# Decoding the second network's weights one unit at a time over the experts, its last matrix inside the second network, and the experts' token transposes in two PSUM buffers

## The chip, the cores and the metric

One NeuronCore of one Trainium2 chip runs the whole program. The metric is the device time of one execution in microseconds (us). The engines are PE (TensorE, matrix products), DVE (VectorE), ACT (ScalarE), POOL (GpSimd) and SP, which here only issues DMAs. SBUF is the on-chip memory, PSUM the memory that PE writes, in banks of 512 floats per partition.

## The reference, cut to what matters

```python
for t in range(S):                                     # gated linear attention, 4 x 8 heads, 768 tokens
    state = alpha[:, :, t, :, None] * state + outer(k[:, :, t], v[:, :, t])
    y[:, :, t] = q[:, :, t] @ state
x = y as 3072 rows of 384
chosen = x @ w_skip > 0                                # only these rows go to an expert
e_idx = argmax(x @ w_gate); gate_w = its softmax       # one of 8 experts
x[chosen] += gate_w * (relu(x @ w1[e]) @ w2[e])        # 384 -> 1024 -> 384
h = maximum(maximum(x @ w1, x @ w2), x @ w3)           # second network, 384 -> 768
return h @ w_out                                       # 768 -> 384
```

All of it is in float32. A product is made of three matmuls, with each operand split into a high and a low part.

## The kernel before

**Three stages.** The first stage (0 to 147.55 us) computes the attention and the routing and scatters the chosen tokens into slots of their experts. The experts' stage (147.55 to 317.14 us) takes 8 experts with 256 slots each. The second network (317.14 us to the end) takes all 3072 tokens in 6 groups of 512.

**The experts' loop** runs over s = 0 to 65. The expert is e = s // 8 and the step in it f = s % 8, called "step 0" to "step 7" here. A step does, in this order in every engine's queue: one generator step of the weight decoding (`mdecs`), the split of the expert weights for the step three ahead (`wsplit`: ACT writes wh, L99; then DVE or POOL writes wl, L100; POOL at steps 1, 3 and 6, DVE at the others), the first product (`gemm1`: 9 matmuls, L618 to L620, into PSUM tile ph; ACT writes hh, L623; DVE writes hl, L624) and the second product of two steps earlier (`gemm2`: 6 matmuls, L636 to L638). At step 1 the `gemm2` of the expert before ends: DVE writes o twice (L645) and POOL scatters it by two indirect DMAs (L646). At steps 4, 5 and 6 `xprep` transposes a third of the next expert's tokens on PE (k = 0, 1, 2; L606, two matmuls), then ACT writes xh (L99) and DVE xl (L100).

**PSUM in this stage**: `ps_t` has one buffer, for the transposes (pt); `ps_h` has three, which ph takes in turn; `ps_o` has two. A new tile waits until the readers of the tile that had its buffer are done. For ph and pt the last reader is the DVE operation that writes hl or xl.

**The decoding.** The four matrices of the second network come as 64-bit integers' words in 8 loads (`mload`, tile rm). Each load holds two units of 128 x 576, so a matrix has four units and there are 16. A unit takes `decode_abs` on ACT (L80), `decode_exp` on DVE (L84, L85), `decode_bits` on DVE (L90, L91), a copy to the high part mh on ACT (L580 or L586) and the low part ml on POOL (L583 or L588). With each expert from 3 on, the two units of one load are decoded over steps 0 to 6, interleaved: exp of the first unit at step 1, its bits at step 2, exp of the second at step 3, its bits at step 4, the copies at 3 and 5, the low parts at 4 and 6.

**The end of the experts.** `select` and `merge` add expert 7's output to the first token group, with three one-hot tiles kept in the rm buffers.

**The second network** does for each group g and slice f (6 of them) `gemm1`: 27 matmuls (L772 to L774) into three ph tiles; ACT copies the first (L787), DVE takes the maximum with the other two (L789), ACT writes hh and DVE hl. Its `gemm2` (12 matmuls, L804 to L806, with the last matrix mh[3], ml[3]) follows one slice later. At slices 2 to 4 `gtr` transposes the next group.

**Routing of the last tokens.** Generators `rA` (4 chunks) and `rB` (2 chunks) are advanced by `stage`. Their last part sums the softmax on DVE (L394 to L396) and scatters by indirect DMA on POOL (L399).

Of the kernel before, what the change touches and what calls it, by code (L numbers as in the profile page):

```python
# [44 lines left out]
DEC = 3  # L45
LEAD = 3
WS = 5
HALF = 1
XL = 6
XP = 4  # L50
IX = 6
MF = True
ML = 2
FIRST = (0, 6, 2)
KEEP = (0, 6)
GT = 512
# [7 lines left out]
def tile_gla_moe_moe2(ctx, tc, akq, vp, rp, wgt, cst, io, ew, md, out):  # L64
# [14 lines left out]
    def decode_abs(t, raw):  # L79
        A.activation(t, words(raw)[1], AF.Abs)  # L80
# [21 lines left out]
    with tc.manual_schedule():  # L102
# [427 lines left out]
               ps_s.tile([128, NP, C], F32, name="ps0").rearrange("p a b -> p (a b)")[:, 0:CAP]]  # L530
        gather(0, 3)
        stage(rB)
        gather(3, 4)
        for k in range(k3):
            for m in range(2):
# [1 line left out]
                         start=False, stop=False)  # L537
        stage(rB)
        gather(4, NC)
        stage(rA)  # L540
        stage(rB)
        xs_, xh_, xl_, ix_ = {}, {}, {}, {}
        xh_[0] = xhp.tile([128, k3, CAP], F32R, name="xh")
# [7 lines left out]
        mh = [m2p.tile([128, 2304], F32R, name=f"mh{i}") for i in range(4)]  # L551
        ml = [m2p.tile([128, 2304], F32R, name=f"ml{i}") for i in range(4)]

        ls = ExitStack()
        xp = pool("xp", 2, reuse_waits="tile")
        hq = pool("hq", LAG + 2, reuse_waits="tile")
# [4 lines left out]
        rm = {}  # L561

        def mload(e):
            rm[e] = xp.tile([128, 4 * UN], F32, name="rm")
            SY.dma_start(out=rm[e].bitcast(I32), in_=md[e].bitcast(I32))

        def mdecs(e):
            ts = [xp.tile([128, UN], F32, name="dt") for u in range(2)]
            raw = [rm[e][:, 2 * UN * u:2 * UN * (u + 1)] for u in range(2)]
            zs = [slice((2 * (e % 2) + u) * UN, (2 * (e % 2) + u + 1) * UN) for u in range(2)]  # L570
            h = [mh[e // 2][:, z] for z in zs]
            l = [ml[e // 2][:, z] for z in zs]
            decode_abs(ts[0], raw[0])
            yield
            decode_exp(ts[0])
            decode_abs(ts[1], raw[1])
            yield
            decode_bits(ts[0], raw[0])
            yield
            A.copy(h[0], ts[0])  # L580
            decode_exp(ts[1])
            yield
            G.tensor_tensor(l[0], ts[0], h[0].bitcast(F32), ALU.subtract)  # L583
            decode_bits(ts[1], raw[1])
            yield
            A.copy(h[1], ts[1])  # L586
            yield
            G.tensor_tensor(l[1], ts[1], h[1].bitcast(F32), ALU.subtract)  # L588
            yield

        def xload(e):
            xs_[e] = xp.tile([128, 2, XW], F32, name="xs", bufs=3)
# [2 lines left out]
        def xprep(e, k):  # L595
            xs = xs_[e]
            if k < 0:
                ix_[e] = xp.tile([128, 2, 1], I32, name="ix", bufs=4)
                V.tensor_copy(ix_[e], xs[:, :, DM + 1:DM + 2])
                return  # L600
            if k == 0:
                xh_[e] = xhp.tile([128, k3, CAP], F32R, name="xh")
                xl_[e] = xhp.tile([128, k3, CAP], F32R, name="xl")
            pt = bank(ps_t, "pt")[:, 0:CAP]
            for m in range(2):
                T.transpose(pt[:, m * 128:(m + 1) * 128], xs[:, m, k * 128:(k + 1) * 128], ident)  # L606
            split(xh_[e][:, k, :], xl_[e][:, k, :], pt)
# [65 lines left out]
                         start=(c == 0), stop=False)  # L673

        def select():
            rm_ = [xp.tile([128, 4 * UN], F32, name="rm") for i in range(2)]
            pair = lambda i, a, w: rm_[i][:, a:a + 2 * w].rearrange("p (m d) -> p m d", m=2).bitcast(F32R)
            p7, yh, yl = pair(0, 0, GT), pair(0, 2 * GT, DM), pair(1, 0, DM)
            for m in range(2):
                V.tensor_scalar(p7[:, m, :], iota, xs_[NE - 1][:, m, DM + 1:DM + 2], None, ALU.is_equal)  # L680
            t = rawp.tile([128, 8 * DM], F32, name="raw").bitcast(F32R)
            xh_[0], xl_[0] = (t[:, i * 4 * DM:(i + 1) * 4 * DM].rearrange("p (k t) -> p k t", k=k3) for i in range(2))
            return p7, yh, yl

        def merge():
            e = NE - 1
            p7, yh, yl = sel
            for m in range(2):
                A.activation(yh[:, m], po_[e][m], AF.Copy, scale=xs_[e][:, m, DM:DM + 1])
                V.scalar_tensor_tensor(yl[:, m], po_[e][m], xs_[e][:, m, DM:DM + 1], yh[:, m].bitcast(F32),  # L690
                                       ALU.mult, ALU.subtract)
            for k in range(k3):
                z = slice(k * 128, (k + 1) * 128)
                for i in range(4):
                    T.matmul(pm[k], (yh, yl)[i // 2][:, i % 2, z], p7[:, i % 2, :], start=False, stop=(i == 3))
                split(xh_[0][:, k, :], xl_[0][:, k, :], pm[k])

        xg_ = {}
# [11 lines left out]
            V.tensor_tensor(chk[:, 7:8], chk[:, 5:6], chk[:, 6:7], ALU.mult)  # L710
            V.tensor_copy(okb, chk[:, 7:8])

        if MF:
            mload(0)
        ns = NE * nf1
        dg = [mdecs(e) for e in range(NE)]
        for s in range(ns + LAG):
            e, f = divmod(s, nf1)
            for d in range(NE):
                if s >= d * nf1 + max(DEC - d, 0):  # L720
                    next(dg[d], None)
            if s < ns:
                if 4 <= s + AHEAD < ns:
                    wsplit(s + AHEAD, V if f in (0, 2, 4, 5, 7) or s < 2 else G)
                if s and (s + AHEAD) % 4 == 3 and (s + AHEAD) // 4 + 2 < 2 * NE:
                    wload((s + AHEAD) // 4 + 2)
                if f == XL and e + 2 < NE:
                    xload(e + 2)
                if s == 0:
                    xload(1)  # L730
                    xload(0)
                    if not MF:
                        mload(0)
                if f == ML and e + 1 < NE:
                    mload(e + 1)
                gemm1(s)
            if s in (ns - 1, ns):
                gstart(s - ns + 1)
            if s == ns + 1:
                gstart(2)  # L740
            if s >= LAG:
                gemm2(s - LAG)
            x0 = XP if e else 5
            if e + 1 < NE and x0 <= f < x0 + k3:
                xprep(e + 1, f - x0)
            if f == IX and e < NE:
                xprep(e, -1)
# [48 lines left out]
        def gemm2(g, f):  # L796
# [4 lines left out]
            for c in range(4):  # L801
# [5 lines left out]
                if f == nf2 - 1:  # L807
                    o = xp.tile([128, DM], F32, name="o2", bufs=4)
                    A.copy(o, po)
                    SY.dma_start(out=out[g * GT + c * 128:g * GT + (c + 1) * 128, :], in_=o)  # L810

        pend = None
        for g in range(ng):
            for f in range(nf2):
                gemm1(g, f)
                if f == 0 and g + 1 < ng:
                    gload(g + 1)
                if pend is not None:
                    gemm2(*pend)
                pend = (g, f)  # L820
                if g + 1 < ng and 2 <= f < 2 + k3:
                    gtr(g + 1, f - 2)
# [204 lines left out]
```

## Time and profile before

| what | value |
|---|---|
| median of 3 runs | 637.07 us (636.66 to 638.45) |
| the profiled execution | 631.28 us |
| its span, first to last instruction | 629.5 us |
| PE busy, weight load busy | 591.3 us (94%), 528.4 us (84%) |
| DVE busy | 357.9 us (57%) |
| ACT busy, POOL busy | 242.2 us (38%), 174.8 us (28%) |
| mean granted TensorE clock | 0.987 of full speed |

The profiled execution lies 5.8 us below the median of the runs. Busy shares are means over three stages of different nature, so the rows below are taken by stage, by expert and by step. Times in the rows count from the start of the span. The clock column (PEclk) gives the granted share of 2.4 GHz, so 0.50 is the lower level, 1.2 GHz.

### The profile page before, as it was taken

What the parts mean: (1) busy time and instruction counts of PE and PEld (TensorE: products, weight loads), DVE (VectorE), ACT (ScalarE), POOL (GpSimd) and SP (SyncE); (2) the same over time, 40 slices, a digit from 0 to 9 for tenths busy, and PEclk for the clock granted to TensorE, in tenths of its full rate; (3) what the DMA queues carried; (4) which work ended last, traced back from release to release, by engine and by line L of the source; (5) the groups of instructions that cost most, each with busy time, mean ns of one, the idle gap of its engine ahead of it and who ended that gap; (6) DMA issues with size and microseconds to landing.
All of it is one profiled execution on the core that took longest, in us unless ns stands there. A gap on an engine that the chain in (4) does not pass through costs nothing.

```text
span 629.5 us, 10447 instructions
## 1 busy us (share of the span) xinstructions
PE 591.3 (94%) x4103; PEld 528.4 (84%) x4103; DVE 357.9 (57%) x637; ACT 242.2 (38%) x503; POOL 174.8 (28%) x151
## 2 busy tenths in 40 slices
PE   5999898889798988898999999999999999999995
PEld 3898888789798988898888888888888888888884
DVE  6899999877899888988642323322322332232221
ACT  2556566555455766667221221112212212122111
POOL 5544678735455645664310000000000000000000
PEclk8899999999899999999999999999999999999999
DMA  8689796924875756673130011002003001001001
GB/s 331 241 232 344 265 337 253 367 92 173 290 281 210 282 211 254 221 301 113 56 120 1 1 44 57 1 2 100 1 1 100 1 0 51 1 0 51 1 2 55
DMA packets 28667, 85.67 MB, mean 136 GB/s; under 512 B 3234, under 2 KB 20624, under 8 KB 25664
## 3 DMA queue, kind: packets, MB, share of 16 engines
q1 hardware_dynamic: 26048, 80.08, 36.3%
q0 software_dynamic: 2560, 4.83, 2.0%
q8 instruction: 34, 0.56, 0.4%
q14 instruction: 25, 0.20, 0.1%
HBM read 67.47 MB, written 20.49 MB: 140 GB/s over the span
## 4 chain that ended last, share of the span: by engine, by line
PE 68%; DVE 17%; issue 4%; DMA 4%; POOL 3%; ACT 1%; DVEq 0%; POOLq 0%; ACTq 0%; SPq 0%
PE ph L774 12%; PE ph L773 12%; PE ph L772 12%; PE po L806 4%; PE po L804 4%; PE po L805 4%; DVE dt L85 3%; DVE wl L100 3%; PE ph L619 2%; PE ph L620 2%; PE ph L618 2%; DMA akq<-in_akq_dram 2%; DVE sf L203 2%; PE po L638 2%; PE ps L246 2%
## 5 line engine op out<-in xcount | busy, mean ns | idle before, releaser
L789 DVE TENSOR_TENSOR h<-ph,h 128x512 f32<-128x512 f32 x72 | 49.8, 692 | 173.0 <-PE ph L774 172.9
L772 PE MATMUL ph<-xh,mh 128*128 128x512 f32 x270 | 106.3, 394 | 0.0
L774 PE MATMUL ph<-xh,ml 128*128 128x512 f32 x270 | 105.6, 391 | 0.0
L773 PE MATMUL ph<-xl,mh 128*128 128x512 f32 x270 | 105.4, 390 | 0.0
L99 ACT CAST hh<-h 128x512 fp32r<-128x512 f32 x36 | 22.3, 621 | 150.3 <-DVE h L789 150.3
L100 POOL TENSOR_TENSOR wl<-raw,wh 128x768 fp32r<-128x768 f32 x26 | 48.7, 1872 | 43.7 <-ACT wh L99 41.6
L774 PEld LDWEIGHTS ph<-xh,ml 128*128 128x128 f32 x270 | 50.7, 188 | 10.9
L773 PEld LDWEIGHTS ph<-xl,mh 128*128 128x128 f32 x270 | 50.7, 188 | 9.9
L772 PEld LDWEIGHTS ph<-xh,mh 128*128 128x128 f32 x270 | 50.7, 188 | 9.7
L619 PE MATMUL ph<-xl,wh 128*128 128x256 f32 x192 | 55.2, 288 | 2.4 <-DVE xl L100 2.3
L618 PE MATMUL ph<-xh,wh 128*128 128x256 f32 x192 | 57.2, 298 | 0.0
L99 ACT CAST wh<-raw 128x768 fp32r<-128x768 f32 x64 | 53.4, 834 | 8.4 <-PE po L638 7.8
L620 PE MATMUL ph<-xh,wl 128*128 128x256 f32 x192 | 55.1, 287 | 0.0
L787 ACT COPY h<-ph 128x512 f32<-128x512 f32 x36 | 21.1, 587 | 74.3 <-PE ph L774 74.3
L806 PE MATMUL po<-mh,hl 128*128 128x384 f32 x144 | 48.6, 338 | 0.0
L804 PE MATMUL po<-mh,hh 128*128 128x384 f32 x144 | 48.4, 336 | 0.0
L805 PE MATMUL po<-ml,hh 128*128 128x384 f32 x144 | 48.4, 336 | 0.0
L638 PE MATMUL po<-wh,hl 128*128 128x384 f32 x128 | 44.2, 345 | 0.5 <-DVE hl L624 0.5
L636 PE MATMUL po<-wh,hh 128*128 128x384 f32 x128 | 43.9, 343 | 0.0
L637 PE MATMUL po<-wl,hh 128*128 128x384 f32 x128 | 43.7, 341 | 0.0
L246 PE MATMUL ps<-q,k 64*128 64x128 f32 x384 | 31.7, 292 | 12.5 <-POOL q L221 9.8
L100 DVE TENSOR_TENSOR wl<-raw,wh 128x768 fp32r<-128x768 f32 x38 | 40.7, 1070 | 4.5 <-ACT wh L99 4.5
(170 smaller groups left out, 1224.3 us busy)
## 6 DMA issues: line engine op xcount, KB each, us to landing
raw<-in_ew_dram SPq DMA_DIRECT2D x15, 1536.0 KB, 6.2
akq<-in_akq_dram SPq DMA_DIRECT2D x23, 772.5 KB, 6.4
rm<-in_md_dram SPq DMA_DIRECT2D x8, 1152.0 KB, 9.0
vt<-in_vp_dram SPq DMA_DIRECT2D x24, 200.0 KB, 7.1
out_dram<-o SPq DMA_DIRECT2D x24, 192.0 KB, 2.1
xg<-x SPq DMA_DIRECT2D x5, 768.0 KB, 4.8
x<-xr SPq DMA_DIRECT2D x3, 1152.0 KB, 10.7
slots<-zt SPq DMA_DIRECT2D x16, 193.0 KB, 7.8
```

What stands on the lines that cost most here:

```text
L99: A.copy(h, src)
L100: (eng or V).tensor_tensor(l, src, h.bitcast(F32), ALU.subtract)
L618: T.matmul(ph, wh[:, z], xh_[e][:, k, :], start=(k == 0), stop=False)
L619: T.matmul(ph, wh[:, z], xl_[e][:, k, :], start=False, stop=False)
L620: T.matmul(ph, wl[:, z], xh_[e][:, k, :], start=False, stop=(k == k3 - 1))
L638: T.matmul(po, hl[:, zm], wh, start=False, stop=(f == nf1 - 1))
L772: T.matmul(phs[w], mh[w][:, z], xh_[g][:, k, :], start=(k == 0), stop=False)
L773: T.matmul(phs[w], mh[w][:, z], xl_[g][:, k, :], start=False, stop=False)
L774: T.matmul(phs[w], ml[w][:, z], xh_[g][:, k, :], start=False, stop=(k == k3 - 1))
L804: T.matmul(po, hh[:, zm], mh[3][:, z], start=(f == 0), stop=False)
L805: T.matmul(po, hh[:, zm], ml[3][:, z], start=False, stop=False)
L806: T.matmul(po, hl[:, zm], mh[3][:, z], start=False, stop=(f == nf2 - 1))
```

## The change

- `mdecs` goes over single units, four steps each: exp; bits; copy and the next unit's abs; low part. One generator serves units 0 to 11 from s = 3 on, at every s that isn't a multiple of 6. Twelve units (three matrices) are decoded with the experts.
- The last matrix (units 12 to 15) is decoded in the second network, six generator steps behind each `gemm1` of group 0. It needs three slices for its 17 steps.
- rm and dt get a pool of their own that lives to the end (`rmp`); `select` uses four buffers of the weight split instead of rm.
- The transpose of k = 1 takes a buffer of `ps_h` (tile ph) instead of `ps_t`.
- The last part of `rA` (its softmax sum and four scatters) comes before the second `gather` instead of after the third.

```diff
         gather(0, 3)
         stage(rB)
+        stage(rA)
         gather(3, 4)
...
         gather(4, NC)
-        stage(rA)
         stage(rB)
...
+        def mdecs(i0, i1):
+
+            ts = {}
+
+            def begin(i):
+                if i < i1:
+                    if i % 2 == 0 and i // 2 + 1 < 8:
+                        mload(i // 2 + 1)
+                    ts[i] = rmp.tile([128, UN], F32, name="dt")
+                    decode_abs(ts[i], rm[i // 2][:, i % 2 * 2 * UN:(i % 2 + 1) * 2 * UN])
+
+            begin(i0)
             yield
+            for i in range(i0, i1):
+                z = slice(i % 4 * UN, (i % 4 + 1) * UN)
+                t, h, l = ts[i], mh[i // 4][:, z], ml[i // 4][:, z]
+                decode_exp(t)
+                yield
+                decode_bits(t, rm[i // 2][:, i % 2 * 2 * UN:(i % 2 + 1) * 2 * UN])
+                yield
+                A.copy(h, t)
+                begin(i + 1)
+                yield
+                G.tensor_tensor(l, t, h.bitcast(F32), ALU.subtract)
+                yield
...
-            pt = bank(ps_t, "pt")[:, 0:CAP]
+            pt = (bank(ps_h, "ph") if k == 1 else bank(ps_t, "pt"))[:, 0:CAP]
...
-            rm_ = [xp.tile([128, 4 * UN], F32, name="rm") for i in range(2)]
...
+            w_ = [wsl.tile([128, EW], F32R, name=f"w{a}") for a in "hlhl"]
...
-        dg = [mdecs(e) for e in range(NE)]
+        dec = mdecs(0, 12)
         for s in range(ns + LAG):
             e, f = divmod(s, nf1)
-            for d in range(NE):
-                if s >= d * nf1 + max(DEC - d, 0):
-                    next(dg[d], None)
+            if s >= DEC and s % 6:
+                next(dec, None)
...
+        dec = mdecs(12, 16)
         pend = None
         for g in range(ng):
             for f in range(nf2):
                 gemm1(g, f)
+                for _ in range(6 if g == 0 else 0):
+                    next(dec, None)
```

With five units to three experts, the steps at which exp and bits stand differ. For experts 1, 4 and 7 exp is at step 1 and bits at step 2 (experts 1 and 4 have another exp at step 6 and bits at step 7). For experts 2 and 5 exp is at step 3, bits at step 4 and a second exp at step 7. For expert 0 exp is at step 4 and bits at step 5. For experts 3 and 6 bits of the unit before is at step 1, exp at step 4 and bits at step 5.

On DVE, steps 2 to 5 of expert 6 stand in this order before (hl is the second half of ph, xl of a transpose, dt a unit being decoded):

```order
L624 SCALAR_TENSOR_TENSOR hl<-ph,hh 128x256
L84 TENSOR_SCALAR dt<-dt 128x576
L85 TENSOR_SCALAR dt<-dt 128x576
L624 SCALAR_TENSOR_TENSOR hl<-ph,hh 128x256
L90 SCALAR_TENSOR_TENSOR dt<-rm,dt 128x576
L91 SCALAR_TENSOR_TENSOR dt<-rm,dt 128x576
L100 TENSOR_TENSOR wl<-raw,wh 128x768
L624 SCALAR_TENSOR_TENSOR hl<-ph,hh 128x256
L100 TENSOR_TENSOR xl<-pt,xh 128x256
```

The same steps of expert 6 on DVE with the change, where the line numbers are lower by three:

```order
L624 SCALAR_TENSOR_TENSOR hl<-ph,hh 128x256 x2
L81 TENSOR_SCALAR dt<-dt 128x576
L82 TENSOR_SCALAR dt<-dt 128x576
L97 TENSOR_TENSOR wl<-raw,wh 128x768
L624 SCALAR_TENSOR_TENSOR hl<-ph,hh 128x256
L97 TENSOR_TENSOR xl<-pt,xh 128x256
L87 SCALAR_TENSOR_TENSOR dt<-rm,dt 128x576
L88 SCALAR_TENSOR_TENSOR dt<-rm,dt 128x576
L97 TENSOR_TENSOR wl<-raw,wh 128x768
L624 SCALAR_TENSOR_TENSOR hl<-ph,hh 128x256
L97 TENSOR_TENSOR xl<-ph,xh 128x256
```

Exp has moved behind the hl of step 3, and bits from ahead of the hl of step 4 to behind the xl of step 4; the xl of k = 1 reads ph.

On ACT, the first three slices of the second network before:

```order
L787 COPY h_4271<-ph 128x512
L99 CAST hh_4277<-h_4275 128x512
L787 COPY h_4295<-ph 128x512
L99 CAST hh_4319<-h_4317 128x512
L787 COPY h_4351<-ph 128x512
L99 CAST hh_4375<-h_4373 128x512
L99 CAST xh_4391<-pt 128x512
```

The same place on ACT with the change:

```order
L781 COPY h_4242<-ph 128x512
L96 CAST hh_4248<-h_4246 128x512
L77 ACTIVATE dt<-rm 128x576
L585 CAST mh_2216<-dt 128x576
L77 ACTIVATE dt<-rm 128x576
L781 COPY h_4280<-ph 128x512
L96 CAST hh_4304<-h_4302 128x512
L585 CAST mh_2216<-dt 128x576
L77 ACTIVATE dt<-rm 128x576
L585 CAST mh_2216<-dt 128x576
L77 ACTIVATE dt<-rm 128x576
L781 COPY h_4349<-ph 128x512
```

The abs and copies of units 12 to 15 now stand between one slice's hh and the next slice's copy of ph.

## Rows read from the trace of the kernel before

**Rows 1.** The page's chain of work that ended last, by engine.

```profile
PE 68%; DVE 17%; issue 4%; DMA 4%; POOL 3%; ACT 1%; DVEq 0%; POOLq 0%; ACTq 0%; SPq 0%
```

**Rows 2.** Two stages: stretch, its length, each engine's busy us, PEclk, DMA, GB/s.

```profile
147.55:317.14 169.59, 154.17 (x1041) 147.11 (x1041) 144.82 (x228) 100.43 (x183) 88.28 (x58) 0.98 0.58 212
317.14:629.49 312.35, 305.17 (x1465) 263.94 (x1463) 87.46 (x127) 62.40 (x112) 1.97 (x2) 1.00 0.09 30
```

**Rows 3.** The same view: experts 0, 1, 2, 4, and expert 7's first seven steps.

```profile
147.55:165.06 17.51, 16.27 (x116) 15.43 (x115) 14.97 (x23) 11.36 (x22) 10.70 (x9) 1.00 0.59 211
165.06:187.91 22.85, 20.05 (x129) 19.07 (x129) 20.01 (x38) 12.20 (x22) 11.24 (x8) 0.93 0.71 265
187.91:209.96 22.05, 19.45 (x128) 18.90 (x128) 19.61 (x32) 14.17 (x27) 12.13 (x8) 0.92 0.65 239
230.14:250.30 20.16, 18.12 (x127) 17.45 (x127) 17.86 (x28) 12.85 (x24) 11.20 (x7) 1.00 0.66 246
290.64:306.55 15.91, 15.44 (x106) 14.81 (x106) 14.60 (x22) 8.63 (x16) 9.23 (x6) 1.00 0.20 68
```

**Rows 4.** The same view: steps 5 and 6 of expert 4.

```profile
240.93:245.76 4.83, 2.79 (x20) 2.18 (x19) 4.80 (x8) 2.06 (x4) 1.93 (x2) 1.00 0.04 12
245.76:248.09 2.33, 2.33 (x19) 2.30 (x19) 2.26 (x4) 1.49 (x3) 1.28 (x2) 1.00 0.94 280
```

**Rows 5.** Idle time of PE and its weight loads before the transposes, by what ended it.

```profile
  DVE xl L100: 25.4, 15
...
  DMA xs<-slots: 0.9, 1
```

**Rows 6.** Timeline of DVE in expert 4: start, duration, instruction.

```profile
238.02 0.45 DVE L84 TENSOR_SCALAR dt<-dt 128x576 f32<-128x576 f32 x1
238.51 3.69 DVE L85 TENSOR_SCALAR dt<-dt 128x576 int32<-128x576 int32 x1
...
243.90 0.95 DVE L100 TENSOR_TENSOR wl<-raw,wh 128x768 fp32r<-128x768 f32 x1
244.77 0.42 DVE L624 SCALAR_TENSOR_TENSOR hl<-ph,hh 128x256 fp32r<-128x256 f32 x1
245.10 0.42 DVE L100 TENSOR_TENSOR xl<-pt,xh 128x256 fp32r<-128x256 f32 x1
```

**Rows 7.** Timeline of POOL in the same stretch.

```profile
237.28 1.33 POOL L646 DMA_INDIRECT x<-o,ix  x1 [0.30 <-issue]
238.63 1.86 POOL L100 TENSOR_TENSOR wl<-raw,wh 128x768 fp32r<-128x768 f32 x1
240.44 1.43 POOL L583 TENSOR_TENSOR ml<-dt,mh 128x576 fp32r<-128x576 f32 x1
```

**Rows 8.** The decoding, by tile dt: count, ns min/median/max, first and last start.

```profile
L80 ACT ACTIVATE dt<-rm x16: 716/726/743, 151.7 to 292.2; 128x576 f32<-128x576 f32 x16
...
L90 DVE SCALAR_TENSOR_TENSOR dt<-rm,dt x16: 741/746/3101, 158.6 to 303.0; 128x576 int32<-128x576 int32 x16
```

**Rows 9.** The view of rows 2: a pause of PE in expert 2 and what follows it.

```profile
201.19:203.79 2.60, 0.00 (x2) 0.00 (x1) 2.52 (x4) 1.60 (x5) 1.06 (x1) 0.97 0.08 29
203.60:207.00 3.40, 3.21 (x14) 3.21 (x15) 3.15 (x7) 2.06 (x4) 0.29 (x1) 0.50 0.89 286
```

**Rows 10.** Timeline at the end of the first stage: softmax sum, gather, last scatter.

```profile
145.70 0.18 DVE L394 TENSOR_REDUCE sme<-ex 128x4 f32<-128x32 f32 x1
...
145.86 0.30 PEld L519 LDWEIGHTS pk<-p,xq 128*128 128x128 f32 x2
...
153.84 0.97 POOL L399 DMA_INDIRECT slots<-xr,si  x1 [0.31 <-issue]
```

**Rows 11.** Timeline of the second network's first slices: ACT, DVE, then PE.

```profile
324.53 0.62 ACT L99 CAST hh<-h 128x512 fp32r<-128x512 f32 x1 [1.71 <-DVE h L789]
...
325.18 0.69 DVE L100 TENSOR_TENSOR hl<-h,hh 128x512 fp32r<-128x512 f32 x1 [0.69 <-ACT hh L99]
...
329.74 0.33 PE L804 MATMUL po<-mh,hh 128*128 128x384 f32 x1
```

More of the change, by code (lines that the diff above doesn't have):

```diff
@@ L47 @@
 WS = 5
-HALF = 1
 XL = 6
@@ L51 @@
 IX = 6
-MF = True
-ML = 2
 FIRST = (0, 6, 2)
@@ L552, in tile_gla_moe_moe2 @@
         ml = [m2p.tile([128, 2304], F32R, name=f"ml{i}") for i in range(4)]
+        rmp = ctx.enter_context(tc.tile_pool(name="rmp", bufs=2, reuse_waits="tile"))
         ls = ExitStack()
@@ L563, in mload @@
         def mload(e):
-            rm[e] = xp.tile([128, 4 * UN], F32, name="rm")
+            rm[e] = rmp.tile([128, 4 * UN], F32, name="rm")
             SY.dma_start(out=rm[e].bitcast(I32), in_=md[e].bitcast(I32))
[L567 to L573, printed above, removed]
-            yield
[L575 to L589, printed above, removed]
+        def mdecs(i0, i1):
[7 more added lines that the diff above has]
+            begin(i0)
+            yield
+            for i in range(i0, i1):
[10 more added lines that the diff above has]
+                yield
         def xload(e):
@@ L675, in select @@
         def select():
-            rm_ = [xp.tile([128, 4 * UN], F32, name="rm") for i in range(2)]
-            pair = lambda i, a, w: rm_[i][:, a:a + 2 * w].rearrange("p (m d) -> p m d", m=2).bitcast(F32R)
-            p7, yh, yl = pair(0, 0, GT), pair(0, 2 * GT, DM), pair(1, 0, DM)
+            w_ = [wsl.tile([128, EW], F32R, name=f"w{a}") for a in "hlhl"]
+            p7 = [w_[m][:, 0:GT] for m in range(2)]
+            yh, yl = (w.rearrange("p (m d) -> p m d", m=2) for w in w_[2:])
             for m in range(2):
-                V.tensor_scalar(p7[:, m, :], iota, xs_[NE - 1][:, m, DM + 1:DM + 2], None, ALU.is_equal)
+                V.tensor_scalar(p7[m], iota, xs_[NE - 1][:, m, DM + 1:DM + 2], None, ALU.is_equal)
             t = rawp.tile([128, 8 * DM], F32, name="raw").bitcast(F32R)
@@ L694, in merge @@
                 for i in range(4):
-                    T.matmul(pm[k], (yh, yl)[i // 2][:, i % 2, z], p7[:, i % 2, :], start=False, stop=(i == 3))
+                    T.matmul(pm[k], (yh, yl)[i // 2][:, i % 2, z], p7[i % 2], start=False, stop=(i == 3))
                 split(xh_[0][:, k, :], xl_[0][:, k, :], pm[k])
@@ L711, in check @@
             V.tensor_copy(okb, chk[:, 7:8])
-        if MF:
-            mload(0)
+        mload(0)
         ns = NE * nf1
-        dg = [mdecs(e) for e in range(NE)]
+        dec = mdecs(0, 12)
         for s in range(ns + LAG):
             e, f = divmod(s, nf1)
-            for d in range(NE):
-                if s >= d * nf1 + max(DEC - d, 0):
-                    next(dg[d], None)
+            if s >= DEC and s % 6:
+                next(dec, None)
             if s < ns:
@@ L731, in tile_gla_moe_moe2 @@
                     xload(0)
[L732 to L735, printed above, removed]
                 gemm1(s)
```

## The prediction

> **What bounds the kernel now.** I first asked which engine the end hangs on. The chain of waits lies on PE for 68% and on DVE for 17% [rows 1], so somewhere PE waits for DVE. By stages [rows 2], PE is busy for 305.17 of 312.35 us in the second network; the experts' stage has 154.17 of 169.59, with DVE at 144.82. So the 17% is to be sought with the experts. By experts [rows 3], number 4 takes 20.16 us (3, 5 and 6 take 20.18, 20.17, 20.17), numbers 1 and 2 take 22.85 and 22.05. By steps [rows 4], step 5 of expert 4 takes 4.83 us and step 6, with the same number of matmuls, 2.33. So 2.50 us of each ordinary expert is a wait, and an expert without it would take 20.16 - 2.50 = 17.66 us. The views of the transposes name the releaser: 25.4 us of idle time (PE and its weight loads counted separately) end with DVE's xl [rows 5]. With one pt buffer, the transposes of k = 1 wait for the xl of k = 0, which comes at 245.10 [rows 6].
>
> Why is DVE late? Its L85 takes 3.69 us at 238.51, where L84, of the same shape and just ahead of it, takes 0.45 [rows 6]. POOL starts a low part of expert weights at 238.63 and a low part of decoded weights at 240.44, ending at 241.87 [rows 7]; L85 ends 0.3 us after. L90, which reads two tiles, has its own worst case of 3.10 against 0.75 [rows 8]. So these DVE operations stand still while POOL works, across two POOL instructions if these follow one another. That is 3.2 us of DVE time per expert, ahead of the hl of steps 3 and 4.
>
> Two experts lose more. In expert 2 PE pauses for 2.60 us, and from 203.60 to 207.00 the granted clock is 0.50, the 1.2 GHz level [rows 9]; half of 3.4 us, 1.7, is lost again. Expert 1 shows a share of 0.93 for the same reason. The pauses of expert 4 (20.16 - 18.12 = 2.04) leave the clock at 1.00 [rows 3].
>
> **The change part by part.** *The second bank.* The transposes of k = 1 no longer wait for the xl of k = 0, but they take one of the three ph buffers. So the ph of step 6 gets the buffer of step 4 and must wait for the hl of step 4 (before, that of step 3), and the ph of step 7 for the hl of step 5. In expert 4 step 6 could start at 240.93 + 2.33 = 243.26, while the hl of step 4 ends at 244.77 + 0.42 = 245.19 [rows 4, 6]. With the old decoding PE would then still wait 1.93 us at step 6. The bank alone is worth 0.1 us per expert at this place, and what is gained must come from an earlier hl of step 4.
>
> *The spread.* It takes four units out of the stage: four times L84, L85, L90, L91 (0.45 twice and 0.75 twice, 2.4 us, with L85 taken as L84 and L91 as L90 [rows 6, 8]), 9.6 us of DVE. More weighs where the rest stands. Experts 1 and 4 have nothing of a unit between steps 2 and 6. There the wl of step 4 can lose to POOL's wl of step 3, which ends at 240.49, 10.35 us into the expert [rows 7]; then wl (0.95) and hl (0.42) [rows 6] end at 11.7 into the expert, and step 6 needs it at 243.26 - 230.14 = 13.1. No wait. I allow 0.2 for the exp of step 6, which can lose to POOL's third wl ahead of the last xl: 17.9 each. Experts 2 and 5 have exp at step 3 and bits at step 4; bits loses to the same POOL instruction until 10.35, then 1.5 of bits, wl and hl end at 13.2. Taken: 0.25 of wait, 17.9 each. Experts 3 and 6 have exp at step 4, and POOL has the low part of the unit before just ahead of its wl, so exp stands for some 3.2 us as now. What is gained is the bits (1.5 us) that stood ahead of the hl of step 4: it ends 245.19 - 230.14 - 1.5 = 13.55 into the expert, a wait of 0.4. Behind it come xl, bits, wl and hl of step 5 (0.35 + 1.5 + 0.9 + 0.4 = 3.15): 16.7, while step 7 could start at 13.55 + 2.33 = 15.9. A wait of 0.8. So 17.66 + 1.25 = 18.9.
>
> The sum over the experts: expert 1 22.85 to 17.9 (4.9, with its clock), expert 2 22.05 to 17.9 (4.1), experts 3 and 6 1.2 each, experts 4 and 5 2.3 each. Expert 7's first seven steps have 15.91 - 15.44 = 0.5 idle [rows 3]; its exp and bits now stand at steps 1 and 2: 0.5. Together 16.5. The bound on the good side is every wait gone: 5.2 + 4.4 + 4 x 2.5 + 0.5 = 20.1. The bound on the other is 1 us of wait in experts 1, 2, 4 and 5 and 2.5, as now, in 3 and 6: 4.2 + 3.4 + 2 x 1.5 + 0.3 = 10.9.
>
> A page speaks against the 17.9 of experts 2 and 5. Their exp would fall into the span of POOL's indirect DMAs. In the trace L84 ran its normal 0.45 us at 238.02 inside such a span (237.28 to 238.61) [rows 6, 7]. The Trainium skill (SBUF — State Buffer, Who interferes with whom) says that VectorE's fast modes and GpSimd share a port pair under an exclusive lock, descriptor generation included, so that exp or the scatter would have to stand. By the page each would lose up to one 1.33 us span, and the sum would be 2 x 1.3 smaller; the row decides here, and the page's case is inside the range.
>
> *Routing.* The three softmax operations of rA (0.18 each [rows 10]) now stand ahead of rB's rank, 0.55 us on the chain to the last gather; PE reaches that gather at 145.86 with work of its own till then [rows 10]. I take 0.2 lost, 0 to 0.55. The four scatters of rA start some 1.9 us earlier, so the last of six ends at about 152.9 instead of 154.81 [rows 10], and the tokens of expert 1, for which PE waited 0.9 [rows 5], come in time. With a shorter line on DVE at steps 6 and 7 expert 0 gains 1.1 (0.5 to 1.5).
>
> *The second network.* PE has no idle time there to hide in; what hides the decoding is the distance between a slice and its use. ACT ends hh at 325.15, then abs 0.73 to 325.9; DVE ends hl at 325.87 and does exp and bits of unit 12 in 2.4, to 328.4; ACT's copy, taken as long as abs, 0.7, to 329.1; POOL's low part 1.43 [rows 7, 8, 11], to 330.6 with the hand-overs. The first `gemm2` starts at 329.74 [rows 11], and its second matmul, 0.17 later, reads that low part: a wait of 0.7 to 0.8. Then ACT does the copies and abs of units 13 to 15 ahead of the third slice's copy of ph. I follow the same durations through DVE (bits 13, exp 14 behind POOL's low part, bits 14): the last abs ends near 341.8, the copy of ph near 342.4, while PE wants that buffer for the fourth slice near 341.4. A wait of 1.0. Together 1.8; the bounds are 0 and, if each of the two hand-overs slips by a further POOL or ACT instruction (1.4 and 0.7), 3.9. Moved loads cost nothing: the last one lands before 317 behind the other traffic, which falls to a DMA share of 0.09 [rows 2].
>
> *select* in other buffers: their last readers on PE are a step or more back, 0.
>
> **The sum.** 16.5 + 1.1 - 0.2 - 1.8 = 15.6 us gained. Against the profiled execution: 631.28 - 15.6 = 615.7. The runs' median lies 5.8 above that execution, and I keep this distance: 637.07 - 15.6 = 621.5. The bounds are 10.9 + 0.5 - 0.55 - 3.9 = 7.0 and 20.1 + 1.5 = 21.6, so 615.5 to 630.1.
>
> **The rivals.** *The wait only moves.* If exp or bits still loses to two POOL instructions ahead of the hl of step 4 in every expert, PE waits at step 6 as it did at step 5. Experts 3 to 6 stay at 20.17, 1 and 2 fall to that without the clock's loss (2.7 + 1.9), expert 0 gains 0.5, and 2.0 go elsewhere: 637.07 - 3.1 = 634.0. For it: the 1.93 above and three buffers for four users. Against it: four of six experts have no exp at step 4. On a second buffer the Trainium skill (TensorE: Matmul & The Clock Gate, HAM oscillation) reports a kernel in which PSUM double-buffering gave no further gain; no run here shows that.
>
> *The second network pays.* If the two waits there are 3.9 and one of them is as long as the pause of rows 9, 1.7 of clock comes on top: 5.6. With 12 gained from the experts the result is 637.07 - 6.4 = 630.7. For it: PE has no slack there. Against it: both waits are worked out at 1 us or less.
>
> *Slower.* If step 6 waits for the hl of step 4 over 2.3 us, as expert 2's pause did, the clock falls after it each time, and an expert takes 22.05 as expert 2 does [rows 3]. Six of these are 132.3 against 125.6 now: 6.7 lost, with the second network 8.5: 645.6. It decides at an hl of step 4 that ends 13.1 + 2.3 = 15.4 us into the expert; now it ends at 15.05, and the change takes work from ahead of it. That speaks against it.
>
> **How the numbers follow.** The forecast has 0.64, the moved wait 0.14, the paying second network 0.16, slower 0.06. A measurement of this kernel tells a change over 0.3% (1.9 us) from none. Of the moved wait's case a third would lie within that: faster 0.89, same 0.05, slower 0.06. The range takes the forecast's bounds and most of the second network's case: 615.0 to 631.0.
>
> **What would show it.** Right: in the profile after, L85's line (82) has fewer long cases, the transposes' idle time for xl goes from 25.4 to a few us, no stretch at 0.50 stands in the experts' stage, experts 1, 2, 4 and 5 take 17.7 to 18.2 us and 3 and 6 about 19, with their wait at steps 6 and 7 ended by hl. In the second network two PE waits of about 1 us stand in the first four slices, for ml and for a copy of ph. Wrong: a wait of 2 us at step 6 of every expert, or waits of over 2 us in the second network.

## The result and the profile after

The changed kernel takes 628.64 us (median of 4 runs, 627.51 to 630.5) beside 636.87 us (4 runs, 634.66 to 638.45) for the kernel before: a ratio of 0.9876 with a 95% interval of 0.9838 to 0.9914, 8.2 us gained. The forecast was 621.5, 15.6 gained, with a range of 615.0 to 631.0. Direction and range held; about half of the forecast gain did not come.

The profiled execution of the changed kernel took 628.60 us, with a span of 626.8 us. That is 2.7 us less than the profiled execution before, whose time lay below its median. The chain of waits after, by engine, beside [rows 1]:

```profile
PE 71%; DVE 18%; issue 4%; ACT 3%; POOL 2%; DMA 0%; another core or an unknown queue 0%; DVEq 0%; POOLq 0%; ACTq 0%
```

PE's share rose by 3 points only, and DVE still holds 18% of the chain. The view by stretches shows where: first the two stages, beside [rows 2], then experts 0, 1, 2, 3 and 4 and expert 7's first seven steps, beside [rows 3]. Columns: stretch, length, busy time of PE, weight loads, DVE, ACT, POOL, then PEclk, DMA share, GB/s.

```profile
152.75:313.16 160.41, 151.37 (x1041) 146.75 (x1041) 130.58 (x212) 93.69 (x175) 82.02 (x52) 0.99 0.61 223
313.16:626.80 313.64, 305.71 (x1465) 264.05 (x1463) 98.10 (x143) 67.10 (x120) 7.67 (x6) 1.00 0.09 30
...
152.75:173.21 20.46, 17.95 (x115) 16.97 (x115) 14.38 (x23) 10.97 (x22) 10.04 (x7) 0.92 0.65 235
173.21:191.51 18.30, 18.22 (x129) 17.77 (x128) 14.81 (x32) 11.65 (x22) 9.93 (x6) 0.99 0.70 248
191.51:209.63 18.12, 18.06 (x128) 17.56 (x128) 16.29 (x30) 12.22 (x23) 10.95 (x7) 1.00 0.59 211
209.63:230.96 21.33, 18.23 (x127) 17.64 (x127) 20.51 (x28) 12.51 (x23) 10.84 (x7) 1.00 0.69 266
230.96:248.65 17.69, 17.69 (x127) 17.59 (x127) 14.42 (x25) 11.48 (x21) 10.52 (x6) 1.00 0.72 266
287.65:302.58 14.93, 14.93 (x107) 14.93 (x106) 11.49 (x20) 7.34 (x13) 7.97 (x5) 1.00 0.30 108
```

The experts' stage fell from 169.59 to 160.41. Expert 4 takes 17.69 and has PE busy all the time (the forecast was 17.9, with 0.2 of wait), and so does expert 5 (17.67). Experts 3 and 6 (both 21.33) are *slower* than before (20.18 and 20.17), and expert 0 went from 17.51 to 20.46, with a clock of 0.92. The first stage, too, ends later: at 152.75 instead of 147.55.

What PE waits for, first in the experts' stage, then in the first slices of the second network (waited for, us in total, times, longest):

```profile
PE ph L618 <- DVE hl L624: 8.5, 5, 2.3
...
PE po L799 <- POOL ml L588: 0.5, 1, 0.5
PE ph L766 <- ACT h L781: 0.5, 1, 0.5
```

The transposes no longer wait for xl [rows 5]; all that is left is five waits of ph for hl, the ring of three buffers. They are one in expert 0 and two each in experts 3 and 6. DVE and POOL in expert 3, which begins at 209.63, in the form of [rows 6, 7]:

```profile
213.07 2.31 DVE L88 SCALAR_TENSOR_TENSOR dt<-rm,dt 128x576 int32<-128x576 int32 x1
...
215.64 1.13 DVE L645 SCALAR_TENSOR_TENSOR o<-po,xs 128x384 f32<-128x384 f32 x2
...
219.12 3.77 DVE L81 TENSOR_SCALAR dt<-dt 128x576 f32<-128x576 f32 x1
...
224.17 0.42 DVE L624 SCALAR_TENSOR_TENSOR hl<-ph,hh 128x256 fp32r<-128x256 f32 x1
...
224.83 1.85 DVE L87 SCALAR_TENSOR_TENSOR dt<-rm,dt 128x576 int32<-128x576 int32 x1
...
228.27 0.42 DVE L624 SCALAR_TENSOR_TENSOR hl<-ph,hh 128x256 fp32r<-128x256 f32 x1
```

```profile
212.92 1.85 POOL L97 TENSOR_TENSOR wl<-raw,wh 128x768 fp32r<-128x768 f32 x1 [3.83 <-ACT wh L96]
...
217.82 1.48 POOL L646 DMA_INDIRECT x<-o,ix  x1 [0.30 <-issue]
219.31 1.45 POOL L588 TENSOR_TENSOR ml<-dt,mh 128x576 fp32r<-128x576 f32 x1
220.71 1.86 POOL L97 TENSOR_TENSOR wl<-raw,wh 128x768 fp32r<-128x768 f32 x1
224.24 1.83 POOL L97 TENSOR_TENSOR wl<-raw,wh 128x768 fp32r<-128x768 f32 x1 [1.68 <-ACT wh L96]
```

Read it from the top. The bits of step 1 meet POOL's first wl and stand until 215.38. The next hl and the two o come after them, so POOL's second scatter begins at 217.82, and its pair of low parts runs from 219.31 to 222.57, 9.7 to 12.9 us into the expert. In expert 4 before it was 8.5 to 11.7 [rows 7]. The exp, at 219.12, stands through the whole pair. The hl of step 4 ends 14.96 us into the expert, against 13.55 forecast. Then the bits stand behind POOL's third wl, and the hl of step 5 ends at 228.69, 19.06 into the expert against 16.7.

The steps in which these waits lie: steps 5 and 6 of expert 3, each of which takes 2.33 where PE does not wait [rows 4]. PE is idle for 1.62 us in the first and 1.49 in the second.

```profile
222.70:226.91 4.21, 2.59 (x19) 2.31 (x18) 4.14 (x7) 1.49 (x3) 1.83 (x1) 1.00 0.38 93
226.91:231.00 4.09, 2.60 (x19) 2.37 (x18) 4.09 (x9) 2.68 (x5) 1.43 (x1) 1.00 1.01 410
```

### The profile page after: what moved, and what is told of

It reads as the page before. It is cut to its first block, busy times and chain, and to the rows that moved or that the text cites. A ratio compares the mean times of both kernels' runs of the same rounds, so it can differ in the third digit from the quotient of the medians.

```text
span 626.8 us, 10450 instructions
## 1 busy us (share of the span) xinstructions
PE 592.0 (94%) x4102; PEld 530.2 (85%) x4103; DVE 354.3 (57%) x637; ACT 239.9 (38%) x503; POOL 175.7 (28%) x151
## 4 chain that ended last, share of the span: by engine, by line
PE 71%; DVE 18%; issue 4%; ACT 3%; POOL 2%; DMA 0%; another core or an unknown queue 0%; DVEq 0%; POOLq 0%; ACTq 0%
PE ph L766 11%; PE ph L768 11%; PE ph L767 11%; PE po L800 4%; PE po L798 4%; PE po L799 4%; PE ps L243 3%; DVE sf L200 3%; PE ph L618 2%; DVE wl L97 2%; PE po L638 2%; PE ph L619 2%; PE ph L620 2%; DVE ap L214 2%; PE po L636 2%
## 5 line engine op out<-in xcount | busy, mean ns | idle before, releaser
L97 DVE TENSOR_TENSOR wl<-raw,wh 128x768 fp32r<-128x768 f32 x38 | 42.6, 1120 | 8.8 <-ACT wh L96 8.5
L618 PEld LDWEIGHTS ph<-xh,wh 128*128 128x128 f32 x192 | 36.9, 192 | 10.2 <-DVE hl L624 10.0
```

The costliest lines, as they stand in the source:

```text
L97: (eng or V).tensor_tensor(l, src, h.bitcast(F32), ALU.subtract)
L618: T.matmul(ph, wh[:, z], xh_[e][:, k, :], start=(k == 0), stop=False)
```

## The experiments

The runs were made on three chips (A, B, C), with the kernel before timed beside them: 636.14 us on A, 633.51 on B, 632.48 on C. Ratios below are to these runs, each with its 95% interval; they are not exactly the quotients of the medians. Line numbers are those of the changed kernel unless said.

**The decoding at other steps.** The theory: experts 3 and 6 are slow because exp stands at the one step where POOL has a pair of operations in front of it; at other steps it costs nothing. In even experts exp, bits, copy and low part go to steps 3 to 6, in odd ones one unit to steps 1, 2, 3, 5 and the next to 6 and 7.

```diff
-            if s >= DEC and s % 6:
+            if s >= 2 and (s == 2 or s > 2 and f in ((0, 1, 3, 4, 5, 6), (1, 2, 3, 5, 6, 7))[e % 2]):
                 next(dec, None)
```

> The changed kernel with other steps for the decoding: the even experts have exp at step 3, bits 4, copy 5, low part 6, the odd ones exp 1, bits 2, copy 3, low part 5, exp 6, bits 7, and the rest at steps 0 and 1 of the next; both buffers of the transposes kept. So no exp stands at step 4 behind a low part. Theory (lock): every expert from 1 to 6 takes 17.6 to 18.2 us, 7 us less than the changed kernel in experts 3 and 6 together, expert 0 under 18.5. Rival (ring alone): the waits of 1.5 us at steps 6 and 7 stay in some experts, 21 us.

Measured: 617.84 us, 0.9699 (0.9657 to 0.9740). Expert 3 by the view of stretches, then exp by its tile over the whole run (count, ns min/median/max):

```profile
205.34:223.04 17.70, 17.70 (x127) 17.59 (x127) 15.12 (x26) 11.48 (x21) 10.53 (x6) 1.00 0.81 303
```

```profile
L81 DVE TENSOR_SCALAR dt<-dt x16: 444/451/2010, 158.9 to 329.3; 128x576 f32<-128x576 f32 x16
```

The same work, with the same three ph buffers, leaves PE no pause in experts 3 and 6 (17.70). No exp of 3.77 is left; the one of 2.01 stands in expert 0, which takes 18.64 and so just misses the 18.5 expected. On the same chip the unaltered changed kernel had 21.35 and 21.33 in experts 3 and 6:

> The changed kernel unaltered, once more. Theory (lock): experts 3 and 6 take 21.3 us again, with PE waits of about 1.6 and 1.5 us at steps 6 and 7, and experts 4 and 5 take 17.7. Open: whether expert 0 takes 20.5 us again (a pause of 2.4 us on ACT before the hh of its step 1 and a PE wait of 2.3 us at step 7) or less, and whether the first stage ends at 152.8 us again or near the 147.6 of the kernel before. If the first stage is only a matter of the run, it differs here by some us with the same instructions.

The unaltered kernel took 626.72 us, 0.9846 (0.9802 to 0.9889), with the same two exp of 3.77, so the first result repeats.

**The bank taken back**, with the new decoding and with the other steps:

```diff
-            pt = (bank(ps_h, "ph") if k == 1 else bank(ps_t, "pt"))[:, 0:CAP]
+            pt = bank(ps_t, "pt")[:, 0:CAP]
```

> The changed kernel with the transposes of k = 1 back in the single pt buffer. Theory (lock): exp of experts 3 and 6 still stands 3.8 us behind POOL's low part and weight split; PE then waits about 2.0 us before the transposes of k = 1 and little at steps 6 and 7, so these experts take 19.7 to 20.3 us instead of 21.3, and the ring of three has made them dearer. Rival (ring alone): with the old pt buffer the waits vanish, 17.7 us. Experts 4 and 5 stay at 17.7 to 18.3 by both. Whole kernel against the changed one: lock -1 to -3 us, ring -7.

> The kernel with the other decoding steps, and the transposes of k = 1 back in the single pt buffer. Theory (lock): the second buffer matters only where the xl of k = 0 is late; in the odd experts it is not (17.7 us), in the even ones, with bits at step 4, xl ends about 13.5 us into the expert where PE wants it at 12.9: 0.3 to 0.8 us of wait, 18.0 to 18.5. In all 1 to 3 us more than with two buffers. Rival (the second buffer is what pays): every expert waits about 2 us again, 19.7 or more.

Measured: 625.51 us, 0.9829 (0.9787 to 0.9871), and 619.72 us, 0.9732 (0.9692 to 0.9772). Experts 3 and 4 of the first of them:

```profile
208.07:227.10 19.03, 18.12 (x127) 17.45 (x127) 15.70 (x25) 12.03 (x22) 10.68 (x7) 1.00 0.72 273
227.10:245.68 18.58, 17.90 (x127) 17.51 (x127) 16.47 (x24) 11.69 (x23) 10.41 (x7) 1.00 0.69 256
```

With the decoding spread as the change spreads it, the bank is no gain as a whole: it takes 0.9 us from each of experts 4 and 5 (18.58 to 17.67), some 0.5 from each of 1 and 2, and gives 2.3 back in each of 3 and 6 (19.03 to 21.33). There the first matmul of ph waits for a late hl over the ring, for longer than the transposes waited for xl without the bank. Expert 0 takes 20.68 without the bank and 18.71 with it, but a stretch at a clock of 0.50 stands in the first of these executions only, so this difference can't be put down to the bank. The expectation of 19.7 to 20.3 for experts 3 and 6 without the bank was too high, that of 17.7 to 18.3 for 4 and 5 too low; the rival's 17.7 did not come either. With the other steps the bank gains 1.9 us (619.72 to 617.84; each run with it is below each without), 0.4 to 0.5 in each of experts 1, 2, 4 and 6 by the profiles.

**The bank alone**, on the kernel before:

```diff
-            pt = bank(ps_t, "pt")[:, 0:CAP]
+            pt = (bank(ps_h, "ph") if k == 1 else bank(ps_t, "pt"))[:, 0:CAP]
```

> The kernel before, with the transposes of k = 1 in a ph buffer and nothing else changed. Theory (the bank does not remove the wait while the old decoding stands ahead of the hl of step 4): the wait of 2.5 us moves from step 5 to the start of step 6 and is about 1.9 us there, ended by hl; experts 3 to 6 take 19.5 to 20.2 us (20.17 before); the whole is within 3 us of the kernel before. Rival (the bank itself is what brings the gain of experts 4 and 5): they fall to 17.7 to 18.2.

Measured: 630.12 us, 0.9950 (0.9921 to 0.9979). Expert 4:

```profile
231.06:250.72 19.66, 18.19 (x128) 17.55 (x128) 17.84 (x28) 12.69 (x24) 11.33 (x7) 1.00 0.69 254
```

19.66 against 20.17: the wait of 2.02 is now one of 1.47 at step 6, for hl. So the bank is worth 0.5 us per expert by itself. The decoding by itself (the run without the bank) brings these experts to 18.58, 1.6 less, and both together to 17.67. So the gain of experts 4 and 5 (2.5) comes from both parts, the most of it from the decoding, as the prediction had it.

**Two low parts later.** In experts 3 and 6 POOL's low part of the unit before is issued behind POOL's third wl instead of ahead of its second (helper lines are 6 higher here).

```diff
+                while late:
+                    G.tensor_tensor(*late.pop())
                 A.copy(h, t)
...
-                G.tensor_tensor(l, t, h.bitcast(F32), ALU.subtract)
+                if i in (4, 9):
+                    late.append((l, t, h.bitcast(F32), ALU.subtract))
+                else:
+                    G.tensor_tensor(l, t, h.bitcast(F32), ALU.subtract)
```

> The changed kernel, with POOL's low part of the unit that stands ahead of POOL's second wl in experts 3 and 6 issued behind that expert's third wl, so that POOL's pair of operations is no longer back to back where exp stands. Theory (DVE's exp stands as long as POOL works without a pause): the two exp operations of 3.77 us fall to 2.2 to 2.5, the wait at step 6 of experts 3 and 6 falls from 1.6 to below 0.4, that at step 7 may stay near 1; these experts take 18.5 to 20.0 (21.33 unaltered). Rival (three ph buffers for four users set the time of these two experts): unchanged at 21.3.

Measured: 622.08 us, 0.9822 (0.9777 to 0.9866), not told from the changed kernel on the other chips (0.9832 to 0.9876; it was not run on chip B). Experts 3 and 6 take 21.41 and 20.47, above the 18.5 to 20.0 expected. The timeline of DVE and POOL in expert 3, which begins at 201.87:

```profile
211.35 2.40 DVE L81 TENSOR_SCALAR dt<-dt 128x576 f32<-128x576 f32 x1
...
215.03 0.42 DVE L630 SCALAR_TENSOR_TENSOR hl<-ph,hh 128x256 fp32r<-128x256 f32 x1
...
217.15 2.58 DVE L97 TENSOR_TENSOR wl<-raw,wh 128x768 fp32r<-128x768 f32 x1
219.65 0.41 DVE L630 SCALAR_TENSOR_TENSOR hl<-ph,hh 128x256 fp32r<-128x256 f32 x1
```

```profile
216.48 2.43 POOL L97 TENSOR_TENSOR wl<-raw,wh 128x768 fp32r<-128x768 f32 x1 [3.06 <-ACT wh L96]
218.88 2.13 POOL L587 TENSOR_TENSOR ml<-dt,mh 128x576 fp32r<-128x576 f32 x1
```

The first half of the expectation held: with a pause of POOL behind it exp takes 2.40 instead of 3.77, the hl of step 4 ends 13.6 into the expert, and the wait at step 6 is 0.2. The second did not: DVE, now earlier, meets POOL's third wl with its own wl of step 5, which takes 2.58, and the wait at step 7 grows to 2.01. The last 0.8 us of this wl lie beside the low part that this edit itself put there. So neither side holds for the whole expert: exp's length is set by POOL's pair, but freeing it alone only moves DVE into the next meeting. In expert 3 the clock falls after that pause, in expert 6 it stays at 1.00 after one as long (2.0). The stretch in expert 3 (PEclk third from the end):

```profile
221.18:224.59 3.41, 3.41 (x16) 3.41 (x15) 2.75 (x4) 2.43 (x4) 1.22 (x1) 0.50 0.99 406
```

**The earlier part of rA alone**, on the kernel before:

```diff
         stage(rB)
+        stage(rA)
         gather(3, 4)
...
         gather(4, NC)
-        stage(rA)
```

> The kernel before, with only the earlier place of the last part of rA. Theory: the last of the scatters starts about 2 us earlier relative to the start of the experts' stage, the wait of 0.9 us for expert 1's tokens goes, and the whole gains 0 to 1 us. If the pause of ACT ahead of the hh of step 1 of expert 0 (1.7 to 2.4 us in every kernel with the change, not in the one before) comes from this part, it stands here too; if it comes from the decoding or the loads, it does not.

Measured: 631.95 us, 0.9981 (0.9948 to 1.0014): not told from no change. Within the profile expert 0 takes 15.96 instead of 17.5 and PE's wait for expert 1's tokens is gone. But experts 3 and 4 take 21.7 each in this execution, since the clock fell to 0.50 after their usual pauses of 2.02:

```profile
221.12:223.14 2.02, 0.00 (x0) 0.00 (x1) 2.02 (x5) 1.55 (x3) 0.81 (x1) 1.00 0.00 0
224.65:228.06 3.41, 3.41 (x15) 3.31 (x15) 1.44 (x6) 1.56 (x4) 1.82 (x1) 0.50 0.96 399
```

**Expert 0: both kernels with a profile on one chip.** In the profile after and in all four of chip A, ACT paused for 1.7 to 2.4 us ahead of the hh of step 1 of expert 0. Within 129 to 135 us DVE, and ACT which waited for it, paused for some 3 us. The profile of before shows no such pauses. These are ACT's hh of step 1 in the profile after, and in the changed kernel on chip C:

```profile
158.39 0.38 ACT L623 ACTIVATE hh<-ph 128x256 fp32r<-128x256 f32 x1 [2.43 <-PE po L638]
```

```profile
150.20 0.38 ACT L623 ACTIVATE hh<-ph 128x256 fp32r<-128x256 f32 x1
```

> The kernel before, unaltered, for a profile on the same chip as the changed one. Theory (the pauses of ACT near 135 us and ahead of the hh of step 1 of expert 0 belong to the chip of a run, not to the change): both kernels show the two pauses, or both show none; with them the experts' stage begins at 150 us or later, and expert 0 takes 18.5 or more; without them it begins below 149.5. Rival (the change brings the pauses): this kernel shows none, the changed one beside it shows both.

> The changed kernel, unaltered, beside the kernel before. Theory: as said for before_2. If this chip shows no pauses, expert 0 takes 16.0 here, as in the run with other places for two low parts, and the forecast of 1.1 us gained in expert 0 was right; experts 3 and 6 take 21.3 either way; the whole is 0.982 to 0.988 of before.

Measured on chip C: the changed kernel takes 621.37 us, 0.9832 (0.9802 to 0.9863), and neither kernel shows the pauses. The kernel before has 630.44 in these runs beside 632.48 in the others on that chip (0.9981, the same kernel), which is how far two sets of runs can lie apart. The two stages of the kernel before, and its expert 0:

```profile
146.70:315.97 169.27, 153.04 (x1041) 145.64 (x1041) 144.83 (x228) 100.42 (x183) 89.93 (x58) 0.99 0.58 212
315.97:628.60 312.63, 305.19 (x1465) 263.97 (x1463) 87.43 (x127) 62.39 (x112) 1.97 (x2) 0.99 0.09 30
...
146.70:164.18 17.48, 16.29 (x115) 15.44 (x115) 14.94 (x23) 11.35 (x22) 10.81 (x9) 1.00 0.58 209
```

The same of the changed kernel, with expert 3 as well:

```profile
147.41:304.00 156.59, 149.34 (x1042) 145.30 (x1042) 128.57 (x212) 93.99 (x175) 80.99 (x52) 1.00 0.62 229
304.00:619.10 315.10, 305.70 (x1465) 263.99 (x1463) 98.08 (x143) 67.07 (x120) 7.66 (x6) 0.99 0.09 29
...
147.41:163.36 15.95, 15.88 (x115) 15.56 (x115) 11.14 (x21) 10.80 (x21) 8.61 (x7) 1.00 0.68 255
200.47:221.80 21.33, 18.23 (x128) 17.65 (x127) 20.50 (x28) 12.52 (x23) 10.83 (x7) 1.00 0.70 267
```

Expert 0 gains 1.5 here, and the experts' stage 12.7. So the pauses are not in the changed program as such: they came in the first profile after and on chip A, and not in the changed kernel and its variants on B and C. Whether the kernel before has them where the changed one has them, no run shows: it was not profiled on A, and the chip of the first profiles is not on record. That its time, too, is 3.7 us longer on A than on C fits that. What the pauses are stays open.

**The second network.** Five steps of its decoding ahead of its first product, on top of the other steps:

```diff
         dec = mdecs(12, 16)
+        for _ in range(5):
+            next(dec)
         pend = None
```

> The kernel with the other decoding steps (sched), and the first five steps of the second network's decoding issued ahead of its first product instead of behind it. Theory: the waits of 0.55 and 0.47 us for ml and for the copy of ph vanish, group 0 takes 49.6 us as before the change (51.1 with it), the whole is 1.2 to 1.5 us below sched: 616.3 to 616.6 against 617.84. Rival (the extra work on DVE and ACT only delays the first slice itself): group 0 stays at 51 or more.

Measured: 614.72 us, 0.9699 (0.9654 to 0.9743), the same ratio as without. Group 0 takes 50.90 instead of 51.12: the wait for ml is gone, but ACT's copy to mh stands at 303.18 behind the bits, the copy of the first ph comes after it, and PE waits 0.58 for that. The theory (49.6) fell; the rival (the first slice itself is late) is nearer, though its 51 is just missed. The two runs are of different chips, so whether the 0.2 shows in the time can't be told.

In the last run one generator goes over all 16 units. Step 7 of expert 6 and steps 0 and 4 of expert 7 take a decoding step too, so that the first unit of the last matrix is done but for its low part when the second network begins. There four steps follow each `gemm1` instead of six.

```diff
-        dec = mdecs(0, 12)
+        dec = mdecs(0, 16)
...
-            if s >= DEC and s % 6:
+            if s >= 2 and (s == 2 or s >= 55 or s > 2 and f in ((0, 1, 3, 4, 5, 6), (1, 2, 3, 5, 6, 7))[e % 2]):
...
-        dec = mdecs(12, 16)
...
-                for _ in range(6 if g == 0 else 0):
+                for _ in range(4 if g == 0 else 0):
```

> The other decoding steps (sched), expert 7 and the two steps behind it taking a decoding step each, so that exp, bits and copy of the first unit of the last matrix are done before the second network, and there four steps behind each first product instead of six. Theory (the two waits of the second network are hand-overs of ACT and POOL that come late because the 17 steps are packed into three slices): no wait over 0.3 us in group 0, which takes 49.6 to 49.9 us as before the change; the experts 3 to 6 stay at 17.7; the whole is 0.966 to 0.968 of before, against 0.970 for sched. Rival (any decoding in the second network costs, as in the run with five steps ahead of its first product): group 0 stays at 50.9 or more.

Measured: 612.28 us, 0.9678 (0.9657 to 0.9698), as expected: 20.2 us below the kernel before and 9.1 below the changed one on the same chip. Group 0 by the view of stretches, then all waits of PE from the first expert to the end of the second network's first slices:

```profile
297.96:347.51 49.55, 49.55 (x236) 42.10 (x235) 23.66 (x37) 12.44 (x21) 7.73 (x6) 1.00 0.11 39
```

```profile
PE po L638 <- DVE hl L624: 0.8, 2, 0.5
PE ph L618 <- DVE hl L624: 0.4, 1, 0.4
```

Both waits lie ahead of the second network. 49.55 is what group 0 took before any decoding stood in it, so the 13 decoding steps left there are hidden. Expert 7 pays 0.95 us for the added steps (15.88 for its first seven, against 14.93): there a bits operation meets POOL's low part and wl back to back and takes 3.78 us, the same meeting at a new place. Of the two edits in this run, the one that thins the steps out (four instead of six) and the one that has the first unit ready, neither was run alone.

## Why the prediction was right, and where its size was off

Gains in us, term by term: the forecast, the first pair of profiles, and the pair on chip C.

| term | forecast | first pair | chip C |
|---|---|---|---|
| expert 0 | 1.1 | -3.0 | 1.5 |
| expert 1 | 4.9 | 4.6 | 4.4 |
| expert 2 | 4.1 | 3.9 | 3.1 |
| experts 3 and 6 | 2.4 | -2.3 | -2.3 |
| experts 4 and 5 | 4.6 | 5.0 | 5.0 |
| expert 7 | 0.5 | 1.0 | 1.0 |
| second network, group 0 | -1.8 | -1.6 | -1.6 |
| sum of these | 15.8 | 7.6 | 11.1 |
| first stage (routing) | -0.2 | -5.2 | -0.7 |
| second network behind group 0 | 0 | 0.3 | -0.9 |
| sum, the change of the profiled span | 15.6 | 2.7 | 9.5 |

The medians moved by 8.2 and, on chip C, by 11.1. Each profile is one execution, so these sums explain the medians only in part, and that the sum above the routing comes near them is luck. Of the 5.2 us of the first stage some 3 are the pause of DVE and ACT ahead of 135 us; behind it the clock was 0.50 from 135.90 to 139.31.

**Experts 3 and 6 are the failed step**: "exp stands for some 3.2 us as now. What is gained is the bits (1.5 us) that stood ahead of the hl of step 4". It took the end of POOL's pair from expert 4 before (11.7 into the expert) and kept it, although it also put bits at step 1, just where POOL's first wl runs. These bits stood for 2.31 instead of 0.76, which, by the order of the rows, moved o, the scatters and POOL's pair by 1.2 us, and the bits of step 5 stood too, for 1.85. The forecast waits of 0.4 and 0.8 became 1.62 and 1.49, with the rest of the 3.65 us over 17.7 lost in the same two steps. The term was mis-sized by 4.7 us, as large as the whole shortfall of the terms up to group 0 on chip C (15.8 to 11.1); the other differences cancel there. The other steps of the first experiment take it back, which shows the cause to be the place of exp and bits, not their amount. Which of the two meetings, the one at step 1 or the one at step 4, weighs more was not tried apart.

**Expert 0**: the forecast of 1.1 held where ACT did not pause (1.5), and the run with rA's part alone shows that it comes from there: 15.96 too. That run has the old decoding, so the shorter line on DVE that the prediction named is not needed for it; the reason was wrong in part. In the first profile after, the pause of ACT put the work of ACT and DVE some 2.4 us later while PE went on. Then the hl of step 5 came late, PE paused for 2.34 and the clock fell to 0.50 for the 3.41 us from 170.03 on. That was 4.1 us off the forecast, in a part of the program that no step of it had doubted. The profiles with the pause have 18.6 to 20.7 for expert 0, all of the changed kernel and its variants without it 16.0.

**Experts 1, 2, 4 and 5** came out near what was worked out: 18.30, 18.12, 17.69 and 17.67 against 17.9. On chip C expert 1 took 18.99, with a wait of 0.7 for xl that the forecast does not have. In expert 2 some of the gain forecast was the clock's (1.7): on chip C the kernel before paused there as long (2.59) and kept its clock. It took 21.27 there instead of 22.05, so there was 0.8 less to gain.

**The second bank alone** was put at 0.1 us per expert and is worth 0.5. The sign of the argument held: what the ring asks for (hl of step 4) stayed late with the old decoding.

**The second network**: two waits were forecast, for ml (0.7 to 0.8) and for the copy of ph (1.0). Both are there with the releasers named, 0.55 and 0.49, smaller than forecast. A third cost of 0.5 that was not forecast, in slices of 9.2 and 9.5 us (8.4 and 8.7 before), makes 1.6 in all; that this comes near the 1.8 is in part luck.

**The 5.8 us between the profiled execution and the median** were kept as a distance, and they were none: the profiled execution after (628.60) lies at its median. So the 615.7 worked out for a profiled execution was missed by 12.9 us, the 621.5 for the median by 7.1.

**The rivals.** "The wait only moves" came true in two of six experts, by its own mechanism (exp behind two POOL operations ahead of the hl of step 4), and not in the others. "Slower" needed an hl of step 4 that ends 15.4 into the expert; in expert 3 it ends at 14.96, with a pause of 1.6, and the clock stays at 1.00 there. Its limit of 2.3 us for a pause does not hold: the clock fell after pauses of 2.02 in the run with rA's part alone. "The second network pays" fell.

Of the signs named: experts 3 and 6 take 21.33 instead of about 19, and the two waits of the second network are half of the 1 us named. L82 has no case over 2.01 us (it was L85 with 3.69), but the long ones moved to L81, two of 3.77. The transposes' wait for xl is gone. A stretch at 0.50 stands in the experts' stage of the first profile, though none was to stand there; there is none on chip C.

## What to carry to other kernels

Where two engines exclude one another, moving work by a step is not costed by the work's own length: ask which operation of the other engine it meets at the new place, what it then pushes back there, and whether the meetings repeat. A part with an irregular rhythm (five units to three experts) has to be followed through every phase of it; here two phases of three were costed with care and the third by analogy. And a buffer added to one user of a ring makes the others wait for an older reader: it pays only where that reader is early (here 1.9 us with well placed decoding, nothing as a whole with the change's).

## What the runs showed of the hardware

**DVE's exp stands through POOL operations that follow each other without a pause.** It was 3.77 through a pair and 2.40 with one, for the same unit, and 0.45 where no POOL operation met it. It started, by the trace, 0.19 us ahead of POOL's first operation and stood all the same. The Trainium skill (SBUF — State Buffer, Who interferes with whom) says of VectorE's two-port modes that whoever issues first gets the shared ports for the whole instruction and the other blocks. The blocking agrees; that the operation with the earlier start in the trace is the one that stands, and that exp gets no turn between two of POOL's, is what these rows add. It does not hold for every DVE operation: the wl of 2.58 above ended at 219.73, 0.8 us behind POOL's wl, and it was POOL's low part that took longer then (2.13, against 1.43 elsewhere).

**POOL's indirect DMAs did not hold DVE's exp up.** In the changed kernel on chip C exp of expert 2 takes its normal time inside such a span, as in [rows 6, 7]:

```profile
190.25 0.44 DVE L81 TENSOR_SCALAR dt<-dt 128x576 f32<-128x576 f32 x1
```

```profile
189.33 1.52 POOL L646 DMA_INDIRECT x<-o,ix  x1 [0.16 <-issue]
```

So the lower sum that the prediction worked out from the Trainium skill for experts 2 and 5 did not come about. The scatters themselves vary: 1.52 here and 0.97 for the next one in the same expert. How much of that is exp's is not shown.

**A pause of PE does not decide alone whether the clock falls.** After pauses of 2.02 us in experts 3 and 4 it fell to 0.50 for 3.41 us in the run with rA's part alone, and it stayed at 1.00 through the same pauses of the kernel before on chip C, where expert 4 takes 20.17. There a pause of 2.59 left it at 1.00, after which in the first profile of before it fell [rows 9]:

```profile
200.84:203.43 2.59, 0.00 (x1) 0.01 (x1) 2.53 (x4) 1.59 (x5) 1.05 (x1) 1.00 0.10 36
203.43:206.84 3.41, 2.97 (x21) 2.65 (x22) 3.16 (x6) 2.06 (x4) 0.49 (x1) 1.00 0.92 303
```

So the 1.7 us that such a fall costs (half of 3.41) should stand in a forecast with a chance, not as a term.
